# A transformer block in one kernel: two maxima in the first step of each attention unit, sums copied by VectorE, eight more staged groups of maxima

## The chip, the core and the metric

One core of a Trainium2 chip runs the whole program. The core has five engines that work side by side, each through its own list of instructions: TensorE (PE, matrix products; its weight loads are shown as PEld), VectorE (DVE), ScalarE (ACT), GpSimd (POOL) and SyncE (SP), which here issues most of the DMA transfers between DRAM and the on-chip memory SBUF. Matrix products go to banks of PSUM, which the kernel uses as tiles of 128 x 512 float32. Engines wait for each other at semaphores. The metric is the device time of one execution in microseconds.

## The reference

A pre-norm transformer block on 2048 tokens of width 640, in float32: attention with 32 heads of width 20, then a gated feed-forward part of width 1728.

```python
def _A_ref(x, wqkv, wo):
    B, S, D = x.shape                      # 1, 2048, 640
    H = 32
    Dh = D // H                            # 20
    qkv = (x @ wqkv).reshape(B, S, 3, H, Dh).transpose(2, 0, 3, 1, 4)
    q, k, v = qkv[0], qkv[1], qkv[2]
    scores = jnp.einsum("bhqd,bhkd->bhqk", q, k) * (Dh ** -0.5)
    p = _softmax(scores, axis=-1)
    o = jnp.einsum("bhqk,bhkd->bhqd", p, v)
    return o.transpose(0, 2, 1, 3).reshape(B, S, D) @ wo

def _B_ref(x, w_gate, w_up, w_down):       # widths 640 -> 1728 -> 640
    return (_silu(x @ w_gate) * (x @ w_up)) @ w_down

h = x + _A_ref(_layernorm(x), wqkv, wo)
return h + _B_ref(_layernorm(h), w_gate, w_up, w_down)
```

## The kernel before

The program runs in three stages: projections (normalisation, queries, keys, values), attention, and the output projection with the feed-forward part. Only the first two are touched.

**Attention.** The 32 heads form 8 groups g of four heads, the 2048 queries form 4 chunks c of 512. A *unit* is u = 4 g + c, so there are 32 units. A unit walks over the keys in 16 *steps* kt of 128 keys (loop at L1382 to L1455); 512 steps in all. In a step TensorE computes the scores of the four heads (`scores`, L1302), ScalarE takes their exponential (L1313), and two steps later TensorE multiplies the result with the values and adds it up in a PSUM bank `acc` (`weigh`, L1315). The bank is one of a kind: the next unit's sums start in it after the finished ones have been copied to SBUF (`row_sums`, L1325), which happens in step 1 of the next unit, on ScalarE, between two exponentials.

Softmax needs the maximum of each row of scores before the exponential is taken. These maxima come from a second set of products, with queries and keys the other way round: `max_one` (L267) takes one product of 128 queries by 512 keys for one head and lets VectorE reduce it (L280). A full unit needs 64 of these single maxima (4 key chunks kc, 4 query tiles t, 4 heads). They are made in one long list (`rest`, L341; `singles`, L1360), units in order, for units ahead of the one whose scores are being computed; the list is drawn from at three per step until it is used up. When a unit's maxima are complete, they are turned and stored by DMA into two spare rows of that unit's query tile, so that the score product subtracts them (`max_parts`, `max_turn`, `max_load`, `max_finish`).

A step's work is written out by a string: `W` the weighted sums of the step before the last, `s` and `S` a score product, `m` and `M` a single maximum; small letters use rows 0 to 63 of the array (b = 0), capitals rows 64 to 127 (b = 1). Two strings take turns (`ORDER`, L41).

The query tile of unit u + 3 is loaded in step 6 of unit u, into the place of unit u - 1 (four tiles, L1420). The keys of the next group are loaded, one chunk each, after steps 8, 10, 12 and 14 of a group's second unit (L1424). SP issues these loads in the order of the program, between stores of prepared feed-forward weights (`prepare_weights`, `w_d<-stage`) and the small transfers for the reciprocals (`r<-o`, `r_d<-r`, `rb<-r_d`).

**Maxima in the projections.** Some maxima are not in that list: `in_projections` (L333) says which. They are made during the projections, four at a time by `max_four` (L226): the difference of two halves of the keys (four products of 256 columns), a relu on ScalarE in place (L251), four more products on top, and two reductions on VectorE (L261). The queries and keys for them are read back from DRAM into tiles `raw` (`staged`, L444; `load_items`, L402). The list `early` (L457 to L466) holds these groups in their order; a planner (`visit`, L488) keeps a clock for each engine and puts a group's two halves between the halves of the projection products (`rounds`, L636) where its clocks say that there is room. Maxima take PSUM banks from a ring of five in this stage. What is left in `early` when the projections are written out follows behind them in a loop (L942).

The maxima of a unit are held in tiles `mx` (`mxs`, L200): those with a part made in the projections have their own, the others take turns in three.

## Time and profile before

| | us |
|---|---|
| median of three runs | 2013.42 (2012.51 to 2014.43) |
| the profiled execution | 2012.49 |
| its span, first to last instruction | 2010.7 |

The busy time of the profiled execution by stage: start and end in us, length, then for PE, PEld, DVE, ACT and POOL the busy us and the number of instructions, then the granted clock of TensorE as a share of full speed, the share of the DMA engines and GB/s. The first row is the projections, the second the end of attention, with parts of the output projection in its steps, the third the output projection and the feed-forward part.

```profile
0.00:315.00 315.00, 311.11 (x3513) 294.59 (x3515) 230.72 (x403) 228.47 (x438) 163.26 (x232) 1.00 0.73 231
1342.00:1450.00 108.00, 108.00 (x713) 61.48 (x705) 56.87 (x115) 74.86 (x151) 21.10 (x35) 1.00 0.17 50
1450.00:2010.70 560.70, 555.28 (x2939) 488.06 (x2936) 396.48 (x761) 132.62 (x275) 299.16 (x411) 1.00 0.61 207
```

In the lists of groups, a row reads: line, engine, operation, out<-in, shape, count, then busy us and mean ns of one, then the idle time of the engine in front and what ended it. In a timeline, a row begins with its start and length in us. "Busy" for TensorE counts modelled ends of overlapping matmuls.

```profile
L1313 ACT ACTIVATE probs<-ps_one 128x512 f32<-128x512 f32 x2048 | 1056.0, 612 | 60.6 <-PE ps_one L1307 34.5
L280 DVE TENSOR_REDUCE mx<-ps_max 128x1 f32<-128x512 f32 x1472 | 925.3, 684 | 105.6 <-PE ps_one L1307 77.7
L261 DVE TENSOR_REDUCE mx<-ps_max 128x2 f32<-128x512 f32 x288 | 180.8, 685 | 60.0 <-PE ps_max L239 55.6
L251 ACT ACTIVATE ps_max<-ps_max 128x512 f32<-128x512 f32 x288 | 151.9, 583 | 39.0 <-PE ps_max L239 37.6
```

The count of L280 is the length of the list of single maxima (1472), and half of L261's (288 / 2 = 144) the number of groups of four in the projections.

### The profile page before, as it was taken

The numbers are of one execution on the slowest core, as the hardware profiler recorded it, in microseconds if no ns is written. First come the engines' busy times: TensorE is split into PE (matmuls) and PEld (weight loads), VectorE is DVE, ScalarE is ACT, GpSimd is POOL, SyncE is SP. The second block draws the span as 40 slices with busy tenths as digits, with TensorE's granted clock in tenths as the row PEclk, the third lists the DMA queues.
The fourth block names the chain that finished last, engine by engine and source line by source line (L and its number), as shares of the span: only waits on it lengthen the run. The fifth ranks groups of instructions, "written<-read, shape, count | busy, mean of one in ns | idle before, by whom it ended". The sixth has DMA issues, their size and how long they took to land.

```text
span 2010.7 us, 40033 instructions
## 1 busy us (share of the span) xinstructions
PE 2000.8 (100%) x14353; PEld 1247.0 (62%) x14353; DVE 1603.5 (80%) x2806; ACT 1435.7 (71%) x2818; POOL 796.1 (40%) x1192
## 2 busy tenths in 40 slices
PE   9999999999999999999999999999999999999999
PEld 8999995333333333333333333345598888888888
DVE  5778778898898898988988888886387766676677
ACT  4777778999999999999999999986633222212221
POOL 7564423334443453443500011011156444854555
PEclk9999999999999999999999999999999999999999
DMA  8887562452634544435412122321158654974642
GB/s 252 261 256 262 182 205 77 125 153 89 187 101 142 151 144 129 156 121 177 153 50 77 29 79 64 90 63 58 48 190 301 229 180 161 356 267 158 206 150 93
DMA packets 199580, 310.37 MB, mean 154 GB/s; under 512 B 54016, under 2 KB 88096, under 8 KB 198360
## 3 DMA queue, kind: packets, MB, share of 16 engines
q1 hardware_dynamic: 192792, 284.23, 43.9%
q0 software_dynamic: 6496, 23.60, 4.0%
q8 instruction: 114, 1.87, 0.4%
q14 instruction: 82, 0.67, 0.1%
q10 hardware_dynamic: 96, 0.00, 0.0%
HBM read 208.13 MB, written 99.21 MB: 153 GB/s over the span
## 4 chain that ended last, share of the span: by engine, by line
PE 97%; DVE 1%; DMA 1%; ACT 0%; issue 0%; POOL 0%; SPq 0%; DVEq 0%; ACTq 0%; POOLq 0%
PE acc L1317 25%; PE ps_a L1485 17%; PE ps_one L1307 16%; PE ps_max L274 13%; PE ps_one L645 10%; PE ps_b L1580 9%; PE ps_max L239 3%; PE ps_max L1035 2%; PE ps_b L1035 1%; PE ps_two L698 0%; PE ps_max L1070 0%; DMA o_t<-o_d 0%; DMA m_d<-turned 0%; ACT ps_max L251 0%; PE ps_a L1851 0%
## 5 line engine op out<-in xcount | busy, mean ns | idle before, releaser
L1313 ACT ACTIVATE probs<-ps_one 128x512 f32<-128x512 f32 x2048 | 1056.0, 612 | 60.6 <-PE ps_one L1307 34.5
L280 DVE TENSOR_REDUCE mx<-ps_max 128x1 f32<-128x512 f32 x1472 | 925.3, 684 | 105.6 <-PE ps_one L1307 77.7
L1307 PE MATMUL ps_one<-q_stk,k_stk 62*128 62x512 f32 x2048 | 581.0, 449 | 0.5 <-ACT probs L1313 0.3
L1317 PE MATMUL acc<-probs,v_stk 128*32 128x512 f32 x4096 | 546.3, 604 | 0.0
L1307 PEld LDWEIGHTS ps_one<-q_stk,k_stk 62*128 62x128 f32 x2048 | 248.2, 184 | 440.3 <-ACT probs L1313 414.3
L274 PE MATMUL ps_max<-k_stk,q_stk 60*128 60x512 f32 x1472 | 373.9, 425 | 0.0
L274 PEld LDWEIGHTS ps_max<-k_stk,q_stk 60*128 60x128 f32 x1472 | 272.6, 186 | 23.3 <-DVE mx L280 0.8
L1702 DVE TENSOR_TENSOR tmp<-ps_a,tmp 128x512 f32<-128x512 f32 x208 | 141.3, 690 | 120.6 <-PE ps_a L1485 93.6
L261 DVE TENSOR_REDUCE mx<-ps_max 128x2 f32<-128x512 f32 x288 | 180.8, 685 | 60.0 <-PE ps_max L239 55.6
L1317 PEld LDWEIGHTS acc<-probs,v_stk 128*32 128x32 f32 x4096 | 80.9, 108 | 179.8 <-issue 167.9
L251 ACT ACTIVATE ps_max<-ps_max 128x512 f32<-128x512 f32 x288 | 151.9, 583 | 39.0 <-PE ps_max L239 37.6
L1580 PE MATMUL ps_b<-halves,yp 128*128 128x320 f32 x1032 | 178.7, 308 | 0.2 <-DVE h L1585 0.2
L1580 PEld LDWEIGHTS ps_b<-halves,yp 128*128 128x128 f32 x1032 | 165.2, 188 | 16.0 <-DVE h L1585 0.5
L1485 PE MATMUL ps_a<-t,units 128*128 128x512 f32 x624 | 162.5, 396 | 0.0
L90 POOL TENSOR_TENSOR yp<-y,yp 128x256 fp32r<-128x256 f32 x96 | 60.2, 627 | 187.0 <-ACT yp L89 187.0
L1485 PE MATMUL ps_a<-z,units 128*128 128x512 f32 x516 | 133.9, 394 | 0.0
L1485 PEld LDWEIGHTS ps_a<-t,units 128*128 128x128 f32 x624 | 112.6, 188 | 18.5
L1352 POOL TENSOR_TENSOR o<-o,rb 128x512 f32<-128x512 f32 x31 | 39.8, 1284 | 198.5 <-DMA rb<-r_d 64.5
L1585 DVE TENSOR_TENSOR h<-ps_b,h 128x320 f32<-128x320 f32 x248 | 109.9, 482 | 5.8 <-PE ps_b L1580 4.3
L645 PE MATMUL ps_one<-z_hi,w_lo 64*128 64x512 f32 x380 | 111.8, 392 | 0.0
L645 PE MATMUL ps_one<-z_hi,w_hi 64*128 64x512 f32 x380 | 111.5, 392 | 0.0
L295 POOL CAST neg<-neg 128x16 fp32r<-128x16 f32 x23 | 4.5, 196 | 268.5 <-DVE neg L287 268.5
(220 smaller groups left out, 2749.6 us busy)
## 6 DMA issues: line engine op xcount, KB each, us to landing
units<-w_d SPq DMA_DIRECT2D x186, 256.0 KB
w_d<-stage SPq DMA_DIRECT2D x106, 256.0 KB
halves<-j_d SPq DMA_DIRECT2D x70, 320.0 KB
j_d<-stage SPq DMA_DIRECT2D x42, 320.0 KB
k_stk<-k_d SPq DMA_DIRECT2D x64, 160.0 KB
q_stk<-q_d SPq DMA_DIRECT2D x64, 160.0 KB
raw<-k_d SPq DMA_DIRECT2D x62, 160.0 KB
raw<-q_d SPq DMA_DIRECT2D x54, 160.0 KB
```

What stands on the lines that cost most here:

```text
L251: nc.scalar.activation(ps, ps, AF.Relu)
L261: nc.vector.tensor_reduce(mx[:, b, :, t, kc], ps.rearrange("p (j n) -> p j n", j=2), axis=AX.X, op=ALU.max,)
L274: nc.tensor.matmul(ps, queries[u][rows, pair, t * P : (t + 1) * P], keys[u // NC][rows, pair, kc * CH : (kc + 1) * CH], start=True, stop=True,
L280: nc.vector.tensor_reduce(mxs[u][:, b, pair, t, kc : kc + 1], ps, axis=AX.X, op=ALU.max)
L645: nc.tensor.matmul(ps, a[rows], b[rows], start=(i == n == 0), stop=(i == 1 and n == last), skip_group_check=True,)
L1307: nc.tensor.matmul(ps, keys[u // NC][rows, p, kt * P : (kt + 1) * P], queries[u][rows, p, :], start=True, stop=True,)
L1313: nc.scalar.activation(probs[p][:, b, :], ps, AF.Exp, scale=scale)
L1317: nc.tensor.matmul(acc[32 * j : 32 * j + 32, :], values[u // NC][:, kt, j * VW : j * VW + 32], probs[j // 2][:, j % 2, :], start=(kt == 0) ...
L1485: nc.tensor.matmul(ps.rearrange("p (t n) -> p t n", t=TPC), w[k][:, i], z[k][:, :, j], start=(first and m == 0), stop=(last and m == len(n ...
L1580: nc.tensor.matmul(ps, a, b, start=(n == 0), stop=(n == len(pairs) - 1))
L1585: nc.vector.tensor_tensor(out=h, in0=ps, in1=h, op=ALU.add)
L1702: add = lambda out, ps, x: nc.vector.tensor_tensor(out=out, in0=ps, in1=x, op=ALU.add)
```

## The change

Three edits. First, the first step of every unit but unit 0 uses the string `SHORT`, with two maxima instead of three, as long as the list of single maxima lasts; the two full strings now take turns by a count of their own. Second, the copy of a unit's finished sums goes to VectorE, except for the last unit's. Third, unit 6 joins unit 2 in making its maxima against key chunks 0 and 1 in the projections: eight more groups of four at the end of `early`, 32 fewer single maxima in attention.

```diff
--- before.py
+++ after.py
@@ -39,6 +39,7 @@
 GD = G * DH
 
 ORDER = ("WsSmmSsM", "WSsMMsSm")
+SHORT = "WsSmMsS"
 
 
 @with_exitstack
@@ -197,7 +198,7 @@
     def mx_tile(u, **tag):
         return stk.tile([P, 2, 2, TPC, NC], F32, name=f"mx{u}", **tag)
 
-    mxs = {u: mx_tile(u) for u in range(NU) if u % NC < 2 or u == 2}
+    mxs = {u: mx_tile(u) for u in range(NU) if u % NC < 2 or u in (2, 6)}
 
     clock = dict.fromkeys(("PE", "ACT", "DVE", "POOL"), 0)
     held = [[0] for _ in range(5)]
@@ -333,7 +334,7 @@
     def in_projections(u, kc, t):
 
 
-        return u == 0 or (kc < 2 and (u % NC < 2 or u == 2))
+        return u == 0 or (kc < 2 and (u % NC < 2 or u in (2, 6)))
 
     def moved(u, kc):
         return [t for t in range(TPC) if in_projections(u, kc, t)]
@@ -463,7 +464,7 @@
                 early += staged(0, (0, 2))
             if g == AFTER[1]:
                 early += staged(0, (0, 3))
-        early += staged(0, (2, 1), (2, 0))
+        early += [a for g in (0, 1) for a in staged(g, (2, 1), (2, 0))]
 
         seconds, steps_due = [], [0]
         LANDING, LANDING_FIRST, SLACK, GATE, APART = 8000, 14000, 0, 500, 2500
@@ -1324,7 +1325,10 @@
 
     def row_sums(acc, *queues):
         o = pc.tile([P, CH], F32, name="o", bufs=2)
-        nc.scalar.activation(o, acc, AF.Copy)
+        if len(queues) == 1:
+            nc.vector.tensor_copy(o, acc)
+        else:
+            nc.scalar.activation(o, acc, AF.Copy)
         r = pc.tile([P, 16], F32, name="r")
         for j in range(G):
             queues[j % len(queues)].dma_start(
@@ -1377,7 +1381,7 @@
             queues = [nc.sync] if u + 1 < NU else [nc.scalar, nc.sync]
             tail.append((u, *row_sums(accs.pop(u), *queues)))
 
-    extra = []
+    extra, full_steps = [], 0
     preparing = prepare_weights()
     for u in range(NU):
         g, c = divmod(u, NC)
@@ -1388,7 +1392,13 @@
             now[0] = u * NT + kt
             probs = [pp.tile([P, 2, CH], F32, name="probs") for _ in range(2)]
             heads = [[0, 2], [1, 3]]
-            order = ORDER[now[0] % 2] if singles[0] or singles[1] else "WsSsS"
+            if not (singles[0] or singles[1]):
+                order = "WsSsS"
+            elif kt == 0 and u >= 1:
+                order = SHORT
+            else:
+                order = ORDER[full_steps % 2]
+                full_steps += 1
             for op in order:
                 if op in "mM":
                     next_max(int(op == "M"))
```

TensorE's list at the end of the projections. Rows on L645 (L646 now) are projection products, rows on L239 (L240) the products of a group of four maxima, each row or `x4` being half a group, and L1307 (L1308) is attention's first score. Before:

```order
L645 MATMUL ps_one<-z_hi,w_hi 128x512 x3
L645 MATMUL ps_one<-z_lo,w_hi 128x512 x3
L239 MATMUL ps_max<-raw 128x256 x4
L645 MATMUL ps_one<-z_lo,w_hi 128x512 x2
L645 MATMUL ps_one<-z_hi,w_lo 128x512 x5
L1307 MATMUL ps_one<-q_stk,k_stk_125 128x512 x2
```

Now, from the same place on:

```order
L646 MATMUL ps_one<-z_hi,w_hi 128x512 x3
L646 MATMUL ps_one<-z_lo,w_hi 128x512 x3
L240 MATMUL ps_max<-raw 128x256 x4
L646 MATMUL ps_one<-z_lo,w_hi 128x512
L240 MATMUL ps_max<-raw_157,raw_158 128x256 x4
L646 MATMUL ps_one<-z_lo,w_hi 128x512
L646 MATMUL ps_one<-z_hi,w_lo 128x512 x4
L240 MATMUL ps_max<-raw_157,raw_158 128x256 x4
L646 MATMUL ps_one<-z_hi,w_lo 128x512
L240 MATMUL ps_max<-raw_157,raw_158 128x256 x24
L240 MATMUL ps_max<-raw,raw_158 128x256 x32
L1308 MATMUL ps_one<-q_stk,k_stk_125 128x512 x2
```

The eight new groups are 64 products; 8 stand among the last projection products, 56 between the last of them and attention's first score.

TensorE's list for step 0 of unit 5, with the first row of step 1 behind it: `acc` is `W`, `ps_one` with `q_stk` scores, `ps_max` single maxima. Before:

```order
L1317 MATMUL acc<-probs,v_stk_5633 32x512 x4
L1307 MATMUL ps_one<-q_stk,k_stk_5632 128x512 x2
L274 MATMUL ps_max<-k_stk_5632,q_stk 128x512 x2
L1307 MATMUL ps_one<-q_stk,k_stk_5632 128x512 x2
L274 MATMUL ps_max<-k_stk_5632,q_stk 128x512
L1317 MATMUL acc<-probs,v_stk_5633 32x512 x4
```

Now, the same step:

```order
L1318 MATMUL acc<-probs,v_stk_5759 32x512 x4
L1308 MATMUL ps_one<-q_stk,k_stk_5758 128x512 x2
L275 MATMUL ps_max<-k_stk_5758,q_stk 128x512 x2
L1308 MATMUL ps_one<-q_stk,k_stk_5758 128x512 x2
L1318 MATMUL acc<-probs,v_stk_5759 32x512 x4
```

The maximum behind the second pair of scores is gone from the first step.

TensorE's list in step 7 of unit 7 (`q_stk_7837`, now `q_stk_7946`, are unit 7's queries; `q_stk_8852`, now `q_stk_8970`, unit 9's; `q_stk_9476` unit 10's). Before:

```order
L1307 MATMUL ps_one_9379<-q_stk_7837,k_stk1_5632 128x512
L1307 MATMUL ps_one_9382<-q_stk_7837,k_stk1_5632 128x512
L274 MATMUL ps_max_9385<-k_stk0_125,q_stk_8852 128x512
L274 MATMUL ps_max_9388<-k_stk0_125,q_stk_8852 128x512
L1307 MATMUL ps_one_9391<-q_stk_7837,k_stk1_5632 128x512
```

Now:

```order
L1308 MATMUL ps_one_9490<-q_stk_7946,k_stk1_5758 128x512
L1308 MATMUL ps_one_9493<-q_stk_7946,k_stk1_5758 128x512
L275 MATMUL ps_max_9496<-k_stk0_125,q_stk_8970 128x512
L275 MATMUL ps_max_9499<-k_stk0_125,q_stk_9476 128x512
L1308 MATMUL ps_one_9503<-q_stk_7946,k_stk1_5758 128x512
```

Unit 10's first single maximum has moved here from the start of unit 8; the four loads of its queries stand in the program directly ahead of this step.

## The prediction

> **What bounds the kernel now.** I read the page's chain first, then the busy time by stage, then the rows of a few attention steps.
>
> ```profile
> PE 97%; DVE 1%; DMA 1%; ACT 0%; issue 0%; POOL 0%; SPq 0%; DVEq 0%; ACTq 0%; POOLq 0%
> 315.00:1342.00 1027.00, 1026.41 (x7199) 402.90 (x7199) 919.38 (x1530) 999.71 (x1955) 312.59 (x515) 1.00 0.37 113
> ```
>
> The chain is TensorE almost throughout. The second line is attention up to unit 30 (columns after the stretch: its length, then busy PE, weight loads, DVE, ACT, POOL, then clock, DMA share, GB/s): TensorE never idles, ScalarE and VectorE stand a little below. So a microsecond that TensorE issues less, or waits less, is a microsecond of the total, as long as ScalarE and VectorE keep up. The step shows it (columns: start, length, engine, line; steps 1 to 4 of unit 5, with the copy of unit 4's sums):
>
> ```profile
> 487.64 1.06 PE L1317 MATMUL acc<-probs,v_stk 128*32 128x512 f32 x8
> 488.63 0.50 PE L1307 MATMUL ps_one<-q_stk,k_stk 62*128 62x512 f32 x2
> 488.97 0.40 PE L274 MATMUL ps_max<-k_stk,q_stk 60*128 60x512 f32 x1
> 489.21 0.49 PE L274 MATMUL ps_max<-k_stk,q_stk 60*128 60x512 f32 x2
> 489.44 0.40 PE L1307 MATMUL ps_one<-q_stk,k_stk 62*128 62x512 f32 x1
> 489.77 1.06 PE L1317 MATMUL acc<-probs,v_stk 128*32 128x512 f32 x8
> ...
> 492.04 1.07 PE L1317 MATMUL acc<-probs,v_stk 128*32 128x512 f32 x8
> ...
> 494.18 0.64 PE L1317 MATMUL acc<-probs,v_stk 128*32 128x512 f32 x4
> ```
>
> From one group of weighted sums (L1317) to the next is a step: 2.13 us. After 0.99 us of sums come four places, at 488.63, 488.97, 489.21 and 489.44. Two products that use different halves of the array's rows share a place; seven products, four of them on one half, need four places.
>
> **What the change removes.** Thirty steps (the first of units 1 to 30) hold three pairs, mM between two pairs of scores, and no fourth place. The place from 489.21 to 489.44 goes: 0.23 us each, 30 x 0.23 = **-6.9 us**. ScalarE keeps up: its exps start 0.48 apart (four in 2.07 us below, the last one 0.60 long), so four need 1.92 us, against 2.13 - 0.23 = 1.90 for a short step. The 0.02 is covered by the 0.2 of slack in the next step.
>
> ```profile
> L1327 ACT ACTIVATE o<-acc x31: 598/629/631, 352.1 to 1402.4; 128x512 f32<-128x512 f32 x31
> PEld acc L1317: 10.5, 29
> 487.04 2.07 ACT L1313 ACTIVATE probs<-ps_one 128x512 f32<-128x512 f32 x4
> 488.97 0.63 ACT L1327 ACTIVATE o<-acc 128x512 f32<-128x512 f32 x1
> 489.40 1.89 DVE L280 TENSOR_REDUCE mx<-ps_max 128x1 f32<-128x512 f32 x3 [0.25 <-PE ps_one L1307]
> 315.67 0.69 DVE L732 COPY e<-ps_one 128x512 f32<-128x512 f32 x1 [0.42 <-issue]
> ```
>
> The copy of a unit's sums pushes the exps behind it 0.48 us back, and the step that starts at 489.77 lasts 2.27 us, 0.14 over the others. The second row says that 29 times a weight load for the sums waited for this copy. On VectorE the copy (0.69 by the nearest row, 0.61 as a pitch) takes the place of the missing reduction: it falls due as the two short-step reductions end, and is over some 0.2 us before the next unit's sums want the bank. So 29 x 0.14 = **-4.1 us**; if VectorE came late by its whole pitch beyond the 0.25 us of idle time in each step, 0.36 a unit, 10 us in all, would be given back. Together -11.0.
>
> **What it adds at the end of the projections.** Before, the last four-maxima group ends with seven halves of projections behind it. In the new order two of the eight begin among the last seven, and 56 of their products (14 halves of a group) stand behind the last projection, with nothing between. What paces them:
>
> ```profile
> 311.97 1.08 ACT L251 ACTIVATE ps_max<-ps_max 128x512 f32<-128x512 f32 x2
> 312.33 1.29 DVE L261 TENSOR_REDUCE mx<-ps_max 128x2 f32<-128x512 f32 x2 [1.27 <-PE ps_max L239]
> 315.20 0.39 PE L645 MATMUL ps_one<-z_hi,w_lo 64*128 64x512 f32 x1
> 316.28 1.28 DVE L280 TENSOR_REDUCE mx<-ps_max 128x1 f32<-128x512 f32 x2
> 318.74 0.64 PE L1317 MATMUL acc<-probs,v_stk 128*32 128x512 f32 x4
> ```
>
> The order takes groups in pairs: differences of both, then maxima of both. A pair needs four of five banks, so the second group of a pair waits for the first reduction of the second group before it. Around that ring: products 0.5, two relus 0.5 + 0.58, products again 0.5, a reduction 0.69: 2.8 us a pair, against 4 x 0.61 = 2.4 if VectorE alone set it. After the last projection (issued 315.20 to 315.43) come three such turns and 1.7 us for the last group's relus and maxima: 10.1 us. VectorE then has two reductions left, so attention's first reduction moves from 316.28 to about 327.2, and the first sums (318.74) with it: **+10.9**. Bounds: 2.4 a turn gives 9; 3.2 a turn gives 12.
>
> **What it adds inside attention.** The maxima run ahead. Unit 6 gives 32 of its 64 single maxima to the projections, so later units come 32 places earlier, less one for each short step. Unit 10's first single was number 384 = 8 x 48: unit 8, step 0. Now it is number 352 = 48 + 6 x 47 + 22: unit 7, step 7. But its queries are loaded after unit 7's step 6. One step of margin stands where there were ten. Before, at that step:
>
> ```profile
> 569.15 1.07 PE L1317 MATMUL acc<-probs,v_stk 128*32 128x512 f32 x8
> 570.72 0.52 PE L274 MATMUL ps_max<-k_stk,q_stk 60*128 60x512 f32 x2
> 570.34 1.60 SPq L176 DMA_DIRECT2D q_stk<-q_d  x4
> 577.18 0.39 SPq L1145 DMA_DIRECT2D raw<-in_B_w_gate  x1
> 577.63 0.57 SPq L1145 DMA_DIRECT2D raw<-in_B_w_up  x1
> SPq L1145 <- DMA q_stk<-q_d: 0.5, 1, 0.5
> ```
>
> The four loads are issued from 570.34 on, and SP's next load of weights waits until one of them has landed, at 577.18: 6.8 us after its issue. The second issue (0.4 later) belongs to the same half, so some 577.5. The maximum that needs it stands at 570.72. TensorE works in order, so scores and sums queue behind it, ScalarE and VectorE run dry, and nothing makes it up: **+6.8** (5 to 8). The other half lands about 1 us later, inside the next step.
>
> By the same count unit 14's first single comes in step 9 of unit 11 (number 544 = 48 + 10 x 47 + 26), three steps after the load, and unit 18's in step 10 of unit 15, four after.
>
> ```profile
> 706.16 1.06 PE L1317 MATMUL acc<-probs,v_stk 128*32 128x512 f32 x8
> 707.95 1.86 SPq L176 DMA_DIRECT2D q_stk<-q_d  x4
> 712.12 0.35 SPq L304 DMA_DIRECT2D m_d<-turned  x1
> 718.30 2.80 SPq L314 DMA_DIRECT2D q_stk<-m_d  x4
> 575.70 0.32 SPq L304 DMA_DIRECT2D m_d<-turned  x1
> 579.69 2.75 SPq L314 DMA_DIRECT2D q_stk<-m_d  x4
> 843.21 1.06 PE L1317 MATMUL acc<-probs,v_stk 128*32 128x512 f32 x8
> 843.88 1.50 SPq L176 DMA_DIRECT2D q_stk<-q_d  x4
> 520.78 4.27 SPq L176 DMA_DIRECT2D k_stk<-k_d  x8
> ```
>
> Unit 11's step 7 starts at 706.16; step 9's first maximum falls at 706.16 + 2 x 2.13 + 1.34 = 711.8. The loads start at 707.95, and there the queues are slower: the small store at 712.12 took 6.2 us until its reader could go, the one at 575.70 only 4.0. With 6.8 to 9.0 us, some 8, the first half lands near 716.3: 4.5, and the second half 0.7 more: **+5.2** (3 to 7). Unit 15's step 7 starts at 843.21, the maximum falls at 843.21 + 3 x 2.13 + 1.34 = 850.9, its half (the last two of four) lands near 852: **+1.1** (0 to 2). Unit 8's first keys (number 288: step 2 of unit 6, near 525.3) come from the load issued at 520.78; with 5 to 7 us they land at 526 to 527.5: **+1.2** (0 to 2.5). The other units keep margins of 1.5 us and more by the same working. Stalls: +14.3.
>
> **The sum.** -11.0 + 10.9 + 14.3 = +14.2. The profiled execution took 2012.49 us (span 2010.7), which is 0.93 below the median of 2013.42; on the median the sum is 2027.6.
>
> **A rule that bears on the stalls.** The same 128 x 128 product, repeated at the start of the program:
>
> ```profile
> 2.00:4.00 2.00, 2.00 (x11) 2.00 (x11) 1.00 0.95 317
> 6.00:8.00 2.00, 2.00 (x21) 2.00 (x20) 1.00 1.03 358
> ```
>
> Out of rest TensorE issues half as many in 2 us as 4 us later. If it came out of the two long stalls in this state for some 3 us each, half of that, 1.5 us, would be lost twice: 2030.6. The Trainium skill, page TensorE: Matmul & The Clock Gate, section Part 1: The HAM clock gate, says that the array falls to half its clock after an idle window of about 3.4 us and needs as long a busy one to come back. By that rule the stall of 6.8 us is sure to be followed by slow work and that of 4.5 probably; no row here shows a stop of that length in mid-run. The forecast leaves it out.
>
> **Rivals.**
> 1. *Slow clock after the stalls:* 2030.6, as worked out above. For it: the start. Against it: one start is all that this trace shows.
> 2. *The queries land in time* (not slower). The issue of the loads would have to move ahead, or the transfers take under 2 us: 2027.6 - 14.3 = 2013.3, no difference. It decides at unit 10: the loads must land within 1.6 us of the step's start. Against it: SP issues them behind the spread of the reciprocals and two stores, which stand ahead of them in the new order too, and one landed 6.8 us after its issue.
> 3. *The burst is hidden, and the stalls are small* (faster is reached only so): if TensorE ran attention's scores beside the burst, 8 of the 10.9 would go, and with stalls of 2 the time is 2007. Against it: all 56 products stand ahead of the first score in one in-order queue.
> 4. *The short steps aren't shorter*, because ScalarE's 1.92 us or VectorE's copy rule them: the 6.9 fall away, 2034.5. Against it: 0.2 us of slack in each step on both engines.
>
> **How the numbers follow.** Forecast 0.50; slow clock 0.27; queries in time 0.12; burst hidden 0.04; short steps not shorter 0.07. The predicted time is **2027.6**. Lower bounds of tail (9) and stalls (8): 2019.4; upper bounds of both (12 and 19) with the slow clock: 2036.4. The low end must leave out rivals 2 and 3 (0.16); at the top I stop at 2035. About 0.2% (4 us) is what a measurement of this kernel can tell from no change: forecast, slow clock and rival 4 lie above it, so slower 0.84; rival 2 within it, 0.12; rival 3 below, 0.04.
>
> **What would show it.** In the new trace: starts of unit 1 to 30 with a step of 1.90 and no step of 2.27 behind it; ten microseconds at about 315 to 326 with TensorE partly idle between L240 products; TensorE idle for 5 to 8 us in unit 7's step 7, released by a DMA of q_stk from q_d, for 4 to 6 in unit 11's step 9, and about 1 in unit 15 and early in unit 6. If units 7 and 11 show no such gap, the prediction is wrong by the stalls; if attention starts less than 5 us later than before, by the burst. Matmuls twice as far apart behind a gap would be rival 1.

## The result

The changed kernel takes **2035.22 us** (median of 4 runs, 2034.81 to 2036.65); the kernel before, run beside it, 2013.04 (2012.51 to 2014.43). The ratio is 1.0108, with an interval of 1.0096 to 1.0121: slower by some 22 us. That is 0.2 us above the top of the predicted range (2019 to 2035) and 7.6 us above the predicted time.

The page of the changed kernel: its span, the chain by engine, and the group of the single maxima (idle time of the engine before them at the end):

```profile
span 2033.4 us, 40102 instructions
PE 97%; DMA 1%; DVE 1%; ACT 1%; issue 0%; POOL 0%; SPq 0%; POOLq 0%; DVEq 0%; ACTq 0%
L275 PE MATMUL ps_max<-k_stk,q_stk 60*128 60x512 f32 x1440 | 364.0, 426 | 12.9 <-DMA q_stk<-q_d 12.9
```

The span is 22.7 us longer. A DMA has come into the chain: TensorE stood still for 12.9 us in front of maxima whose queries had not landed. The kernel before had no such wait.

To see where the rest comes from, I took the start of each step's weighted sums (L1317 before, L1318 after) in both traces and subtracted:

| part | before to after, us | predicted |
|---|---|---|
| up to the second weighted sums of unit 0 (320.85 before, 334.18 after) | +13.3 | +10.9 |
| units 1 to 29, without units 7, 11 and 15's late loads | -9.7 | -11.0 |
| unit 7, steps 7 and 8 | +8.7 | +6.8 |
| unit 11, steps 9 and 10 | +7.3 | +5.2 |
| unit 15, step 10 | +1.4 | +1.1 |
| unit 6, keys of unit 8 | 0 | +1.2 |
| units 30 and 31 | +0.2 | 0 |
| behind attention | +1.5 | 0 |

What units 7, 11 and 15 lose is counted against the same units of experiment 1 below, where they wait for nothing. The last row isn't put down to the change. The code behind attention is the same in all kernels here, and from the last weighted sums to the end of the span they took between 559.9 and 565.8 us.

**The burst behind the projections.** TensorE in the changed kernel (columns: start, length, engine, line; the last products of the projections are issued at 315.50):

```profile
315.73 2.57 PE L240 MATMUL ps_max<-raw,raw 60*128 60x256 f32 x11
...
319.58 1.72 PE L240 MATMUL ps_max<-raw,raw 60*128 60x256 f32 x9 [0.20 <-ACT ps_max L252]
321.51 5.91 PE L240 MATMUL ps_max<-raw,raw 60*128 60x256 f32 x27 [0.21 <-DVE mx L262]
327.01 1.25 PE L1308 MATMUL ps_one<-q_stk,k_stk 62*128 62x512 f32 x2
...
331.18 1.93 PE L1318 MATMUL acc<-probs,v_stk 128*32 128x512 f32 x8
```

And VectorE in the same place:

```profile
316.59 2.47 DVE L262 TENSOR_REDUCE mx<-ps_max 128x2 f32<-128x512 f32 x4
319.38 2.68 DVE L262 TENSOR_REDUCE mx<-ps_max 128x2 f32<-128x512 f32 x4 [0.31 <-PE ps_max L240]
322.94 2.48 DVE L262 TENSOR_REDUCE mx<-ps_max 128x2 f32<-128x512 f32 x4 [0.88 <-PE ps_max L240]
326.13 2.48 DVE L262 TENSOR_REDUCE mx<-ps_max 128x2 f32<-128x512 f32 x4 [0.70 <-ACT ps_max L252]
328.53 1.88 DVE L281 TENSOR_REDUCE mx<-ps_max 128x1 f32<-128x512 f32 x3
```

The reductions go in fours, a pair of groups at a time, as the prediction had it. From 316.59 to 326.13 are three turns, on average 3.2 us each, not 2.8. They aren't alike: the first takes 2.79 us, as worked out, the two behind it 3.56 and 3.19. Attention's first reduction (L281) stands at 328.53 instead of 316.28: 12.25 later, where 10.9 was worked out.

**The clock.** Stretches of the changed kernel (columns as in the prediction; the clock is the third from the end):

```profile
316.00:320.00 4.00, 3.17 (x19) 1.83 (x17) 3.69 (x7) 2.78 (x6) 2.66 (x4) 0.93 0.60 152
320.00:324.00 4.00, 3.79 (x23) 2.98 (x23) 3.02 (x6) 2.11 (x5) 0.00 (x0) 0.50 0.77 231
324.00:328.00 4.00, 3.98 (x20) 2.57 (x16) 3.30 (x7) 2.39 (x5) 0.47 (x1) 0.50 0.01 2
...
586.00:589.00 3.00, 0.41 (x2) 0.44 (x4) 0.00 (x0) 0.00 (x0) 0.00 (x0) 0.50 0.54 210
589.00:592.00 3.00, 3.00 (x14) 0.69 (x14) 1.51 (x3) 1.09 (x2) 0.84 (x4) 0.50 0.09 33
```

The granted clock is half in three places: from 319.42 for 13.65 us, in the burst and over the first step of attention; and from 585.65 and 732.43 for 6.83 us each, at the end of the two long stalls and behind them. The last two are the first rival of the prediction. The first one isn't in the prediction at all. It begins 0.04 us behind the end of the burst's first turn; up to there the profile, whose ends of products are modelled, shows no idle gap of TensorE of more than 0.22 us.

**The late queries.** TensorE in unit 7, steps 6 to 9:

```profile
580.16 1.06 PE L1318 MATMUL acc<-probs,v_stk 128*32 128x512 f32 x8
...
581.49 0.39 PE L275 MATMUL ps_max<-k_stk,q_stk 60*128 60x512 f32 x1
588.59 0.76 PE L275 MATMUL ps_max<-k_stk,q_stk 60*128 60x512 f32 x1 [6.71 <-DMA q_stk<-q_d]
...
589.74 1.93 PE L1318 MATMUL acc<-probs,v_stk 128*32 128x512 f32 x8
...
593.12 1.07 PE L1318 MATMUL acc<-probs,v_stk 128*32 128x512 f32 x8
```

The step takes 589.74 - 580.16 = 9.58 us instead of 2.12, and the next one 3.38: its sums last 1.93 instead of 1.06, at half the clock. Of the 8.7 us lost here 6.7 is waiting. The other 2.0 fit the clock: it is at half for 3.89 us behind the stall (588.59 to 592.48), and half of that is 1.95.

### The profile page after: what moved, and what is told of

The parts are those of the page before. It is cut to its first block, busy times and chain, and to the rows that moved or that the text cites. A ratio compares the mean times of both kernels' runs of the same rounds, so it can differ in the third digit from the quotient of the medians.

```text
span 2033.4 us, 40102 instructions
## 1 busy us (share of the span) xinstructions
PE 2009.3 (99%) x14385; PEld 1257.9 (62%) x14385; DVE 1615.4 (79%) x2821; ACT 1432.4 (70%) x2803; POOL 796.9 (39%) x1192
## 4 chain that ended last, share of the span: by engine, by line
PE 97%; DMA 1%; DVE 1%; ACT 1%; issue 0%; POOL 0%; SPq 0%; POOLq 0%; DVEq 0%; ACTq 0%
PE acc L1318 25%; PE ps_a L1495 17%; PE ps_one L1308 15%; PE ps_max L275 12%; PE ps_one L646 10%; PE ps_b L1590 8%; PE ps_max L240 4%; PE ps_max L1036 2%; PE ps_b L1036 1%; DMA q_stk<-q_d 1%; PE ps_two L808 0%; PE ps_two L699 0%; PE ps_max L1071 0%; ACT ps_max L252 0%; DMA rb<-r_d 0%
## 5 line engine op out<-in xcount | busy, mean ns | idle before, releaser
L281 DVE TENSOR_REDUCE mx<-ps_max 128x1 f32<-128x512 f32 x1440 | 906.0, 684 | 112.9 <-PE ps_one L1308 66.7
L1308 PE MATMUL ps_one<-q_stk,k_stk 62*128 62x512 f32 x2048 | 572.0, 449 | 0.2 <-ACT probs L1314 0.2
L1318 PE MATMUL acc<-probs,v_stk 128*32 128x512 f32 x4096 | 548.9, 607 | 0.0
L1308 PEld LDWEIGHTS ps_one<-q_stk,k_stk 62*128 62x128 f32 x2048 | 251.4, 185 | 436.6 <-ACT probs L1314 405.4
L275 PE MATMUL ps_max<-k_stk,q_stk 60*128 60x512 f32 x1440 | 364.0, 426 | 12.9 <-DMA q_stk<-q_d 12.9
L275 PEld LDWEIGHTS ps_max<-k_stk,q_stk 60*128 60x128 f32 x1440 | 262.3, 187 | 36.9 <-issue 12.5
L262 DVE TENSOR_REDUCE mx<-ps_max 128x2 f32<-128x512 f32 x304 | 190.8, 685 | 62.1 <-PE ps_max L240 56.9
L252 ACT ACTIVATE ps_max<-ps_max 128x512 f32<-128x512 f32 x304 | 160.4, 583 | 44.3 <-PE ps_max L240 42.7
L1318 PEld LDWEIGHTS acc<-probs,v_stk 128*32 128x32 f32 x4096 | 81.0, 108 | 175.6 <-issue 167.2
L646 PE MATMUL ps_one<-z_hi,w_lo 64*128 64x512 f32 x380 | 112.1, 392 | 0.0
L646 PE MATMUL ps_one<-z_hi,w_hi 64*128 64x512 f32 x380 | 111.6, 392 | 0.0
L646 PE MATMUL ps_one<-z_lo,w_hi 64*128 64x512 f32 x380 | 110.9, 392 | 0.0
```

The costliest lines, as they stand in the source:

```text
L252: nc.scalar.activation(ps, ps, AF.Relu)
L262: nc.vector.tensor_reduce(mx[:, b, :, t, kc], ps.rearrange("p (j n) -> p j n", j=2), axis=AX.X, op=ALU.max,)
L275: nc.tensor.matmul(ps, queries[u][rows, pair, t * P : (t + 1) * P], keys[u // NC][rows, pair, kc * CH : (kc + 1) * CH], start=True, stop=True,
L281: nc.vector.tensor_reduce(mxs[u][:, b, pair, t, kc : kc + 1], ps, axis=AX.X, op=ALU.max)
L646: nc.tensor.matmul(ps, a[rows], b[rows], start=(i == n == 0), stop=(i == 1 and n == last), skip_group_check=True,)
L1308: nc.tensor.matmul(ps, keys[u // NC][rows, p, kt * P : (kt + 1) * P], queries[u][rows, p, :], start=True, stop=True,)
```

## The experiments

All times stand beside runs of the kernel before on the same chip (2013.0 to 2014.0 in these sittings). Each edit is against the changed kernel unless another is named.

**1. Earlier loads of the queries.** Everything else stays.

```diff
-            if kt == 6 and u + 3 < NU:
+            if kt == 0 and u + 3 < NU:
                 load_queries(u + 3)
```

> The changed kernel with one line moved: the query tile of unit u + 3 is loaded after step 0 of unit u, not after step 6. Nothing else differs. Theory L (the loads come too late because the maxima run ahead): the gaps in unit 7 step 7 (9.58 us against 2.12), unit 11 step 9 (8.33), unit 15 step 10 (3.48) and the slow steps behind them (3.38, 3.22) go, 7.5 + 1.3 + 6.2 + 1.1 + 1.4 = 17.4 us, so 2035.2 falls to about 2018. Rival D (the transfers themselves are slow there, and loading earlier only moves the collision to the small transfers for the reciprocals): less than 10 us come back, 2025 or more, with new waits for r or rb.

Measured: 2018.94 us (2018.26 to 2024.1), ratio 1.0029 (1.0016 to 1.0041). All three gaps are gone, and so are the slow steps behind them; unit 7 is 0.27 us shorter than before like its neighbours. SP issues the loads here at

```profile
568.51 2.39 SPq L177 DMA_DIRECT2D q_stk<-q_d  x4
```

and in the changed kernel at

```profile
581.31 1.60 SPq L177 DMA_DIRECT2D q_stk<-q_d  x4
582.96 10.03 SPq L1117 DMA_DIRECT2D w_d<-stage  x3
```

0.2 us ahead of the maximum that needs them. So the late loads cost 16 us, and the half clock in mid-run was their consequence, not something that came from elsewhere. The half clock of the burst is still there.

**2. Loads after step 4**, the same edit with another number, run twice.

> As the changed kernel, but the loads come two steps earlier (after step 4), 4.3 us. Theory L: the gap in unit 7 shrinks from 7.5 to about 3 us, the one in unit 11 from 6.2 to about 2, the one in unit 15 goes. Theory C (the half clock behind a gap needs a stop of TensorE of more than some 3.4 us): the steps behind the two gaps are back at 2.13, so that together some 12 us of the 17.4 come back, 2023. If the clock fell at any gap, the steps behind would stay at 3.2 to 3.4 and the time would be 2025.

Measured in a single run: 2017.08, with no gap left at all. The expectation counted steps; but the loads also passed the transfers for the reciprocals and the spread that SP issues after step 4, each of which waits for another engine. The remaining 2 to 3 us didn't show up, so this run couldn't tell what a half-late load costs.

> The changed kernel with the loads of queries after step 4 once more, now timed in rounds: 2016 to 2019 by its one look (2017.08) and by the run with the loads after step 0 (2018.94).

Measured: 2019.1 (2018.57 to 2021.51), ratio 1.003 (1.0019 to 1.0042). Here too TensorE waits for no load of queries. One step of unit 11 took 2.96 us, but not for the queries: it is step 13, four steps behind the first use of them, and VectorE stood 1.10 us there for GpSimd's part of a row of maxima (`turned<-neg`, waiting for `neg`).

**3. Idle products in the burst**, to hold the clock up (against experiment 1, idle products that nothing reads). The first version put two products of 128 columns into each pass of the loop that empties the planner's list:

```diff
+        fillers = []
         while behind or early or seconds:
...
             if not behind:
                 finish_splits()
                 slot[0] += 1
+                if not fillers:
+                    fillers.append(ps_one())
+                for _ in range(2):
+                    nc.tensor.matmul(fillers[0][:, :P], ident, ident, start=True, stop=True)
```

> As the run with the loads after step 0, and while the groups of four maxima stand alone behind the last projection, TensorE gets two idle products (128 x 128, into a bank that nothing reads) after each half of a group. They compute nothing that is used. Theory C (part of the 13.3 us by which attention starts later is the clock, which is at half from 319.4 to 333.1): the clock stays full through the burst, the burst ends a microsecond or so earlier although it holds more products, step 0's sums start about 2 us earlier and unit 0's first long step (3.00) is 2.12 again: 2.5 to 3 us less than the run without them. Rival P (the ring of banks alone paces the burst, the clock follows from it and costs nothing): the same time or up to 3 us more for the added products.

Measured: 2034.1, ratio 1.01 (1.0085 to 1.0115). The clock stayed full, but most passes issue no half at all, so up to 20 instructions of filling (2.5 us) stood between two halves and the first score came at 346.75. That says nothing on the cost of the clock. The second and third version put them behind each half:

```diff
+            if idle:
+                for _ in range(2):
+                    nc.tensor.matmul(idle[0][:, :P], ident, ident, start=True, stop=True)
...
         while behind or early or seconds:
+            if not (behind or idle):
+                idle.append(ps_one())
```

> The changed kernel with the loads after step 0, and behind each of the 14 halves that stand behind the projections two idle products of 128 columns (about 0.25 us together by the idle products of the run with too many of them). Theory H (the half clock is an expense of its own): the granted clock stays at 1 through the stretch, first score to first weighted sums takes 3.2 us instead of 4.2, the halves come every 0.6 to 0.7 us instead of 0.85, and the first weighted sums come 2 to 4 us earlier than 332.06; the time is 2015 to 2017. Rival S (the halves wait for ScalarE and VectorE, so that the clock is no matter): the clock stays at 1 and the first weighted sums still come within 1 us of 332.06. Rival N: two products are too little, and the clock falls at the same place as before.

> The changed kernel with the loads after step 0, and one idle product of 96 columns behind each half of the burst (in the run with two of 128 columns TensorE itself took 1.07 us for each half, and hid what the clock is worth). A half and its idle product should now take TensorE about 0.43 + 0.27 us, less than the 0.76 us at which the halves came at full clock (3.05 us for the first four maxima of the burst in the run with early loads). Theory H (the half clock costs time in the burst): the granted clock stays at 1, the halves come every 0.76 to 0.8 us, and the first weighted sums and the step behind them come 2 to 3 us earlier than the 332.06 and 334.54 of the run with early loads. Rival S (ScalarE and VectorE set the pace at either clock): the clock stays at 1, and the second weighted sums come within 1 us of 334.54. Rival N: the clock falls all the same.

(The third has one product of 96 columns in place of the loop.) Measured: 2018.03 (1.0019, 1.0009 to 1.0028) and 2018.68 (1.0032, 1.002 to 1.0043). With two, the clock stays full, but a half and its idle products take TensorE 1.07 us:

```profile
316.79 0.51 PE L242 MATMUL ps_max<-raw,raw 60*128 60x256 f32 x4
317.23 0.71 PE L249 MATMUL ps_one<-ident 128*128 128x128 f32 x4
317.87 0.50 PE L242 MATMUL ps_max<-raw,raw 60*128 60x256 f32 x4
...
330.75 0.50 PE L1316 MATMUL ps_one<-q_stk,k_stk 62*128 62x512 f32 x2
...
334.07 1.06 PE L1326 MATMUL acc<-probs,v_stk 128*32 128x512 f32 x8
```

From the first score to the first sums now takes 3.3 us, where the changed kernel took 4.2, and the step behind is 2.11 instead of 3.00. With one, the burst runs at full clock and the first score comes at 328.52 (327.89 without idle products): the halves come every 0.82 us. TensorE in that run:

```profile
319.93 0.51 PE L242 MATMUL ps_max<-raw,raw 60*128 60x256 f32 x4
320.36 0.46 PE L248 MATMUL ps_one<-ident 128*128 128x96 f32 x2
320.76 0.50 PE L242 MATMUL ps_max<-raw,raw 60*128 60x256 f32 x4
```

A half takes 0.43 us, the idle product behind it 0.40 where 0.27 was expected, and the next half follows at once; between 317 and 328 us TensorE has no idle time. So TensorE with its idle products sets the pace in this run too, and what the half clock costs the burst can't be read from it.

It can be read from the runs without idle products, because the clock doesn't fall at the same point of the burst in all of them. VectorE in experiment 1, where it fell at 319.19:

```profile
317.27 2.48 DVE L262 TENSOR_REDUCE mx<-ps_max 128x2 f32<-128x512 f32 x4
320.32 2.61 DVE L262 TENSOR_REDUCE mx<-ps_max 128x2 f32<-128x512 f32 x4 [0.58 <-PE ps_max L240]
```

| the clock falls | length of the first turn, us |
|---|---|
| 0.04 to 0.34 us behind the end of the first turn (changed kernel, first run of experiment 2, experiments 7 and 9) | 2.79 |
| 1.13 to 1.38 us ahead of it (experiment 1, second run of experiment 2, experiment 6) | 3.05 |

Later turns, which run at half the clock, take 3.2 to 3.6 us (experiment 9 has none). So the clock does bear on the pace of the burst, against rival S. Against the 2.79 of the first turn, the other two of the changed kernel lose 1.2 us at half the clock, by this estimate. With one idle product the clock still falls behind the burst, at 332.55 for 3.41 us, and the first step takes 3.70. In the runs with one and with two the end of unit 0 is 15.3 us later than in the kernel before, against 13.7 without idle products: what they win they cost again, or the fall comes later. Behind the burst the half clock costs 1.2 us in experiment 1 and 1.7 in the changed kernel (first score to second weighted sums 6.65 and 7.17, with the full clock 5.43).

**4. Room for the halves between the projections.** The planner's SLACK from 0 to 200 ns, against experiment 1, leaves 4 products behind the last projection instead of 56.

```diff
-        LANDING, LANDING_FIRST, SLACK, GATE, APART = 8000, 14000, 0, 500, 2500
+        LANDING, LANDING_FIRST, SLACK, GATE, APART = 8000, 14000, 200, 500, 2500
```

> The changed kernel with the loads of queries after step 0, and with the planner's SLACK at 200 instead of 0: a staged half may then be put into the projections' order when the planner's clocks say that its banks come free up to 200 ns later. In the order of the program 4 products then stand behind the last projection instead of 56. Theory T (the tail is the cost of the 14 halves that stand behind the projections): the first weighted sums come near 320 us instead of 332.06, the stretch of half clock at 319 is gone, and the time falls from 2018.9 to 2006 to 2010. Rival P (the halves cost as much between the projections, since TensorE or VectorE is full there): the last projection comes 8 us or more later, and the time stays within 3 us of 2018.9.

Measured: 2029.99 (2028.5 to 2032.69), ratio 1.0076 (1.0059 to 1.0093). The last product of the projections comes at 339.05 instead of 316.18, the first weighted sums at 344.10. The rival is right, and more strongly than it was put: the burst is gone, and the stage is 12 us longer than with it. The order drags over the whole stage: the 1100th of 2100 projection products comes at 181.8 instead of 172.8. The wait that grew is that of TensorE's weight loads for ScalarE's relu: 13.2 us in 58 places between 100 and 340 us, where experiment 1 has 2.3 us in 6 up to 316. No run tests whether that wait alone does it.

**5. The copy alone**: the kernel before with VectorE's copy and nothing else.

```diff
-        nc.scalar.activation(o, acc, AF.Copy)
+        if len(queues) == 1:
+            nc.vector.tensor_copy(o, acc)
+        else:
+            nc.scalar.activation(o, acc, AF.Copy)
```

> The kernel before with one edit of the change: VectorE, not ScalarE, copies the finished sums; three maxima in every step, no added group in the projections. Theory V (the copy needs the place of the missing maximum): VectorE has 0.24 us of idle time per step and the copy takes 0.61, so it ends some 0.35 late once a unit; the 0.15 us that ScalarE's copy cost go, a delay of 0 to 0.35 comes. Between 2009 (all absorbed) and 2019 (0.2 lost a unit, 29 units). If it is at or below 2009.5 the short step isn't needed for the copy; if it is above 2014 it is.

Measured: 2012.77, ratio 0.9994 (0.9985 to 1.0004): no difference. In unit 5 the first three steps take 2.13, 2.17 and 2.22 where the kernel before has 2.13, 2.13 and 2.27: 6.52 and 6.53.

**6. The short step alone**: the copy goes back to ScalarE (experiment 1 with the edit of experiment 5 undone).

> The changed kernel with the loads after step 0 and with ScalarE copying the finished sums again. By the sum of the prediction the copy costs the exponentials 0.14 us in 29 units, 4.1 us: 2023, with one step of each unit at 2.27 instead of 2.13. Rival: a short first step leaves ScalarE no spare time before the copy, and the step behind it costs more than 2.27 (2.4: 2027). Other rival: without the copy on VectorE the short step itself is shorter (1.90) and the two cancel in part (2020).

Measured: 2028.27 (2027.93 to 2030.56), ratio 1.0072 (1.0057 to 1.0087); the first rival. Sums of unit 5's first steps, and ScalarE's copy among its exponentials:

```profile
498.36 1.06 PE L1318 MATMUL acc<-probs,v_stk 128*32 128x512 f32 x8
500.31 1.06 PE L1318 MATMUL acc<-probs,v_stk 128*32 128x512 f32 x8
502.50 1.07 PE L1318 MATMUL acc<-probs,v_stk 128*32 128x512 f32 x8
504.90 1.06 PE L1318 MATMUL acc<-probs,v_stk 128*32 128x512 f32 x8
497.08 4.88 ACT L1314 ACTIVATE probs<-ps_one 128x512 f32<-128x512 f32 x9
501.82 0.63 ACT L1328 ACTIVATE o<-acc 128x512 f32<-128x512 f32 x1
502.30 6.20 ACT L1314 ACTIVATE probs<-ps_one 128x512 f32<-128x512 f32 x12
```

The same unit of experiment 1, with the copy on VectorE in the place that the short step leaves:

```profile
498.02 1.07 PE L1318 MATMUL acc<-probs,v_stk 128*32 128x512 f32 x8
499.96 1.07 PE L1318 MATMUL acc<-probs,v_stk 128*32 128x512 f32 x8
502.10 1.06 PE L1318 MATMUL acc<-probs,v_stk 128*32 128x512 f32 x8
504.24 1.06 PE L1318 MATMUL acc<-probs,v_stk 128*32 128x512 f32 x8
499.78 1.29 DVE L281 TENSOR_REDUCE mx<-ps_max 128x1 f32<-128x512 f32 x2 [0.24 <-PE ps_max L275]
501.10 0.69 DVE L1329 COPY o<-acc 128x512 f32<-128x512 f32 x1
```

Three steps: 504.90 - 498.36 = 6.54 with ScalarE's copy, 504.24 - 498.02 = 6.22 with VectorE's, 6.53 before. ScalarE runs without a break in the first of the two: nine exponentials, the copy, twelve more. Where TensorE's places are one fewer, ScalarE is what is full, and the 0.18 us of the short step are lost again in the two steps behind it (2.19 and 2.40 us). So the short step is worth nothing without the other edit, the other edit nothing without the short step, and both together 0.31 us a unit.

**7. Full first steps** with VectorE's copy, eight staged groups and early loads. (Nothing is computed twice here, otherwise than the expectation says: the list of single maxima stays as short as in the changed kernel, and is used up sooner.)

```diff
-            elif kt == 0 and u >= 1:
-                order = SHORT
```

> The changed kernel with the loads after step 0 and with all first steps holding the same number of maxima as the others (the staged groups are then computed twice, in the projections and in the steps). By the sum of the prediction a short first step is worth 0.23 us in 30 units: 2018.9 + 6.9 = 2025.8. By the run with the copy alone, where the first two steps took 2.18 and 2.22 against 1.95 and 2.13 here, it is 0.32 us in 30 units: 2028.5. Rival: the steps are limited by TensorE's products and not by VectorE's maxima, so that nothing changes: 2019.

Measured: 2024.89 (2023.99 to 2025.24), ratio 1.0052 (1.0037 to 1.0067): 6.0 above experiment 1. Unit 5 loses 0.31 us (2.13 + 2.17 + 2.22 against 1.95 + 2.14 + 2.13), the units 1 to 29 together 10.5, of which 0.9 is a wait at the start of unit 6; unit 30, which has no maxima left to do, gives 4.0 back (51.0 us, 55.0 in experiment 1). That the time lies near the expected 2025.8 is chance: 6.9 was to be lost and nothing to be given back. The 4.0 are what the eight groups bring if short steps don't use it.

**8. Short steps without the groups.** The changed kernel without the eight groups, with short first steps in units 1 to 12 only, and loads as before.

```diff
-        return u == 0 or (kc < 2 and (u % NC < 2 or u in (2, 6)))
+        return u == 0 or (kc < 2 and (u % NC < 2 or u == 2))
...
-        early += [a for g in (0, 1) for a in staged(g, (2, 1), (2, 0))]
+        early += staged(0, (2, 1), (2, 0))
...
-            elif kt == 0 and u >= 1:
+            elif kt == 0 and 1 <= u <= 12:
```

> The kernel before with the copy on VectorE and the short first step in units 1 to 12 alone, and without the eight more staged groups, so that no half stands behind the projections; the 12 maxima that the short steps leave out come in about four more steps of unit 30. Theory (the two edits are worth 0.31 us a unit together, and the staged groups cost more than they bring): the first weighted sums stay at 318.7, units 1 to 12 are 0.31 us shorter each (3.7 us), the four steps cost 0 to 0.44 us more each (0 to 1.8), no query comes late: 2009.5 to 2011.5 beside 2013.4. Rival: the maxima that come later hold up the start of unit 31, which costs 2 to 5 us: 2012 to 2015.

Measured: 2092.5 us, ratio 1.0385 (1.037 to 1.0401). The theory is wrong by some 80 us; the rival named the mechanism, but for one unit, where there were sixteen. Its waits (line, what was waited for: us in total, times, longest):

```profile
PE ps_one L1308 <- DMA q_stk<-m_d: 23.7, 13, 5.3
PE ps_one L1308 <- DMA q_stk<-m: 19.2, 11, 3.4
```

The first scores of a unit wait for the row of its maxima, which comes back to the query tile by DMA. Up to unit 5 the short steps bring their 0.3 us each; unit 6 starts 5.5 us late, and 15 of the later units between 1 and 7. In the order of the list each maximum left out puts off the last one of a later unit by a place, and unit 6, the first to wait, has five such short steps ahead of it. The stalls bring the half clock with them (13 stretches within attention, 3.41 or 6.83 us each). So the groups in the projections are not a third edit beside the other two: they are what pays for the short steps, ahead of time.

**9. Half of it.** Four groups instead of eight, short steps in units 1 to 15, loads after step 4; 6 halves stand behind the projections instead of 14.

```diff
-        return u == 0 or (kc < 2 and (u % NC < 2 or u in (2, 6)))
+        return u == 0 or (kc < 2 and (u % NC < 2 or u == 2 or (u == 6 and t < 2)))
...
-            elif kt == 0 and u >= 1:
+            elif kt == 0 and 1 <= u <= 15:
...
-            if kt == 6 and u + 3 < NU:
+            if kt == 4 and u + 3 < NU:
```

> The changed kernel with loads after step 4, four more staged groups instead of eight (of unit 6, the first two of its four blocks of 128 queries), and short first steps in units 1 to 15 alone: the 15 maxima left out are then covered by the 16 that the four groups hold. In the order of the program 6 halves stand behind the projections instead of 14. Theory (a group costs about 1.7 us in the burst, and the four short steps that it pays for bring 4 x 0.31 = 1.24 us): the first weighted sums come 5 to 6 us later than the 318.74 of before instead of 12 to 13, units 1 to 15 are 0.31 us shorter each (4.7), no unit waits for its row of maxima, and the time is 0.3 to 1.5 us above that of before: 2013.4 to 2014.9 where before is 2013.4. Rival F (most of the tail is a fixed cost, the change from products of projections to those of attention): first weighted sums 9 us late or more, 2017 or more. Rival M (the maxima come too late, as in the run without the groups): stalls for the row of maxima at the start of units, 2020 or more.

Measured: 2013.87 (2012.13 to 2019.98), ratio 1.0005 (0.9996 to 1.0014): no difference from the kernel before. The first sums:

```profile
325.86 1.63 PE L1318 MATMUL acc<-probs,v_stk 128*32 128x512 f32 x8
```

7.1 us later than before (5 to 6 expected, 9 by the rival). Up to the end of unit 0 it is 7.7, against 13.1 (experiment 2, second run) to 13.7 (experiment 1) for 14 halves. By a straight line through the two, an estimate, that is 0.7 us a half, the clock included, and about 3.4 that don't depend on their number. Units 1 to 15 give 5.1 back and the units 16 to 30 another 1.1; no unit waits for its maxima.

## Why the prediction came out as it did

- **Slower: right, and for the reasons given.** The burst and the late queries are there, in the places that were named: the first reduction of attention 12.25 us late, gaps in unit 7 step 7, unit 11 step 9 and unit 15 step 10. Experiment 1 takes the last three away with one line, and 16 us go.
- **The waits themselves were sized well.** 6.7 + 5.1 + 1.1 = 12.9 us of waiting; 6.8 + 5.2 + 1.1 = 13.1 was the working. Unit 7 came out as worked out, from issue (581.31) to landing (588.59). In the other two errors cancel, which is luck. In unit 11 the loads took 9.1 us from the first issue where 8.4 was taken, but the second half cost no wait of its own (0.7 was taken). In unit 15 they were issued 3.4 us behind the start of step 7 instead of 0.7, and took 5.8 us instead of 8. The keys of unit 8 (1.2) came in time.
- **"The forecast leaves it out": this is the step that failed.** The slow clock behind the stalls was put down as a rival with 0.27, at 1.5 us each. It came behind both long stalls, and 2.0 and 2.2 us were lost there beyond the waiting (17.4 us lost in the three units, less 12.9 of waiting, leaves 4.5; 0.3 of it falls in unit 15, where the clock stayed full). The single row at the start of the trace had been taken for too little. The Trainium skill, page TensorE: Matmul & The Clock Gate, section Part 1: The HAM clock gate, has half the clock after an idle window of about 3.4 us; for the stalls of 6.7 and 5.1 us this trace agrees in that the clock fell in both, though in the second already 2.4 us after the last product. Experiment 1 shows the link: without the stalls, no half clock in mid-run. The prediction's own upper bounds with the slow clock gave 2036.4; the top of the range was set at 2035, and the time lies 0.2 above it.
- **The burst was mis-sized: 13.3 for 10.9.** At the full clock the working holds: the first turn took 2.79 us for 2.8. At half the clock the turns took 3.56 and 3.19: +1.2 (experiment 3). The rest, 1.2, is the half clock on attention's first step, 1.7 by experiment 3, less some 0.5 by which the other terms were too large. The prediction spoke of the clock at the stalls alone. (Its lower bound of 9 at 2.4 us a turn should be 9.7 by the same sum, 10.9 - 3 x 0.4, and its upper bounds of the stalls add up to 19.5, not 19; nothing hangs on either.)
- **The gain: -9.7 for -11.0.** In the units 1 to 29 the first step takes 1.95 us instead of 2.14, a gain of 0.19 where 0.23 was taken, and the step of the copy 2.13 instead of 2.27, a gain of 0.14 as taken. The missing 0.04 fit ScalarE: in the short step of unit 5 of experiment 1 its exponentials start without a break 0.48 to 0.49 us apart, and four of them need the 1.95; 1.92 had been reckoned, and slack in the next step was to cover what is over. The prediction let VectorE's copy take the place of the missing reduction, so it had one half of what ties the two edits together. The other half it didn't say: the short step needs the copy off ScalarE. By experiments 5 and 6 each edit alone is worth nothing. The groups' part of the gain, keeping the maxima ahead, had no term at all (experiment 8).
- Together: +2.4 (burst and its clock), +1.3 (gain), +4.5 (behind the stalls, 4.2 of it with the half clock), -0.2 (waits), -1.2 (keys), +0.2 (units 30 and 31) and +1.5 (behind attention) make +8.5 on the predicted 14.2: 22.7, the difference of the spans.

What remains open: why two turns at the same half clock differ by 0.3 to 0.4 us (3.56 and 3.19 in the changed kernel), and whether the wait for the relus is all that slows the projections with SLACK at 200. No version here beats the kernel before by more than can be measured; half of the change (experiment 9) draws level with it.

## What to carry to other kernels

When work is moved ahead of its old time, look up for each of its inputs when the load is issued, not only when it is needed: here the change used up nine of ten steps of margin, and one line that issues the load earlier was worth 16 us. Where two engines are nearly full in the same step, as ScalarE and VectorE are here, look whether relieving one alone gains anything before the parts are added up one by one. Work that fills gaps between other products is cheap only as long as there are gaps; here what was left behind the last of them cost its full length, and the clock fell over it.

## What the runs showed of the hardware

- The clock fell to half without a stop of TensorE. In the changed kernel it fell at 319.42, 3.9 us after the last projection, although by the profile's modelled ends no gap until then was longer than 0.22 us; between 316 and 320 TensorE was busy for 3.17 of 4 us. With one idle product of 96 columns behind each half it stayed full through the whole burst, and fell 4.0 us after the last of them. The Trainium skill, page TensorE: Matmul & The Clock Gate, section Part 1: The HAM clock gate, gives an idle window as the condition; here a thinly filled one was enough.
- Apart from the last one of each run, in which the program ends, the stretches at half clock lasted 3.41, 6.83 or 13.65 us in all these kernels: 1, 2 and 4 times 3.41. With 14 halves in the burst it was 13.65, with 6 halves 6.83. The falls keep that step too: in the changed kernel the second and third come 266.23 and 413.01 us behind the first, 78 and 121 times 3.413. The same section has a window of 3.413 us, which these lengths and distances bear out; that several windows can pass at half clock with TensorE at work is what the traces add.
- In a stall the fall came while TensorE waited (3.8 us after unit 7's last product, 2.4 after unit 11's), and some 4 us of each 6.83 lay behind the stall: 588.59 to 592.48 and 735.13 to 739.26. The third stall, 1.1 us, was followed by none.
